# Two batches of strided attention as 32 by 32 tiles on TensorE, with a softmax of a whole unit at once and 16-bit weight conversion, in an attention and mixer kernel

## The chip, the cores and the metric

The kernel runs on one core of a Trainium2 chip. The metric is the device time of one execution in microseconds (us). Engines are named as the profile names them: PE is TensorE (PEld its weight loads), DVE is VectorE, ACT is ScalarE, POOL is GpSimd, and SP is SyncE, which here issues all DMAs.

## The reference

Eight batches of eight heads, 576 positions, head size 64. Heads 0 to 3 attend locally, heads 4 to 7 with a stride of 32; then a token mixer and a channel MLP.

```python
stride = 32
scores = scale * np.matmul(q, k.transpose(0, 1, 3, 2))
rel = pos[:, None] - pos[None, :]
mask_local = (rel >= 0) & (rel < stride)
mask_strided = (rel >= 0) & (pos[None, :] % stride == pos[:, None] % stride)
...
attn = np.exp(scores)
attn = attn / (np.sum(attn, axis=-1, keepdims=True) + 1e-09)
return np.matmul(attn, v).astype(np.float32)
...
h = np.maximum(xt @ w_tok1, 0.0) @ w_tok2
u = x + h.transpose(0, 2, 1)
h2 = np.maximum(u @ w_ch1, 0.0) @ w_ch2
return (u + h2).astype(np.float32)
```

In a strided head, the positions with the same remainder modulo 32 form a group of 18 that attends only within itself: 32 groups for each head. The weights come as 64-bit floats and are turned into 32-bit ones on the chip.

## The kernel before, in words

**The channel MLP** is most of the work. `mlp` (L450) runs nine groups of 512 tokens. In each, `up_proj(fc)` (L454) does 12 matmuls at L460 for one of 12 feature chunks, ACT makes the high part gh (L463), DVE the low part gl (L464), and `down_proj(fc)` does 12 matmuls at L472. So each product is three matmuls of split numbers (high by high, high by low, low by high), and a group is 288 matmuls. A half step is 12 of them; a group has 24. Other work hangs into the half steps by the table `ins`: the next batch's load of x (`do_load`), the token mixer (`tok1` at L336, `tok2` at L362 and L368), the local attention units of later batches (`late_unit`), the strided attention (`do_strided`), and the pieces of the weights (`do_pieces`).

**Weights.** Each piece goes through `convert` (L79) and `load_split` (L97): a DMA brings 512 KB of 64-bit numbers into one of three `w_raw` buffers; ACT takes the absolute value of the high word, rescaled, into one of two `w_f` buffers (L88); ACT copies one byte of the low word next to the high word (L92, `octets`); DVE shifts and masks (L93) and combines (L94); ACT casts to the high part (L105); POOL subtracts to get the low part (L106). There are 30 conversions: three for w_tok1, three for w_tok2 and 24 for the two channel weights.

**Local attention.** `local_unit` (L125) takes two heads and n chunks of 128 queries. Scores are matmuls of 32 queries by 64 keys (L137). Then for each chunk and head a DVE operation masks and finds the extreme (L146), and ACT takes the exponential with that as bias and sums it up on the way (L149); transposes (L160), the product with v (L167), and a division by the sums (L181). Eight units belong to batches 0 and 1 and run in the first stage, twenty later.

**Strided attention.** Batch 0 is done on PE by `strided_pe` (L217): seven groups of 18 side by side make a block of 126 by 126, of which only the diagonal is kept; per pair of heads there are ten blocks. Batches 1 to 7 are done by `strided` (L271) without PE: POOL multiplies (L286, L303), DVE reduces (L287, L305), 27 operations of each kind and batch. Their results go through DRAM (`xs`) into x.

**The order** is not the program's. The scheduler of the framework, by priorities and a timing model, sets a fixed order for each engine, and each engine then works through its queue in order. The first stage (L403 to L442) has its own pools: the `first` pool, three PSUM buffers each for local and strided work, two for the mixer. `strided` of batch 1 starts there at low priority.

## Time and profile before

| | |
|---|---|
| median of 3 runs | 879.69 us (879.41 to 881.28) |
| the profiled execution's own time | 879.49 us |
| its span, first to last instruction | 877.7 us |
| mean granted TensorE clock | 0.979 of full speed |
| busy: PE, DVE, ACT, POOL | 836.5, 482.7, 268.4, 481.3 us |

A row of groups gives line, engine and operation, what is written and read, its shape and count, then the busy time in us and the mean duration in ns, then the idle time of the engine just ahead of it and who ended it. A row of windows gives the stretch in us, then the busy time and number of instructions of PE, PEld, DVE, ACT and POOL, the granted TensorE clock (PEclk, 1.00 is full speed), the busy share of the DMA engines and GB/s. A row of a timeline starts with the time and the duration in us. Busy times of pipelined matmuls overlap, so their rate is read from the distance of their starts. A float32 matmul appears as two instructions.

### The profile page before, as it was taken

How to read it: one execution, taken by the hardware profiler on the slowest of the kernel's cores; microseconds unless marked ns; L12 is line 12 of the kernel's file. 1: busy time of each engine (PE TensorE's matmuls, PEld its weight loads, DVE VectorE, ACT ScalarE, POOL GpSimd, SP SyncE). 2: the span in 40 equal slices, each digit the busy share in tenths (PEclk: the TensorE clock that was granted, in tenths of full speed). 3: DMA queues.
4: the chain of work that ended last, by engine and by line, in shares of the span. 5: the costliest groups of instructions: out<-in, count | busy, mean ns of one | idle time of the engine just before them, and what ended most of it. 6: DMA issues, size and time to landing. Idle time of an engine off the chain costs nothing.

```text
span 877.7 us, 15029 instructions
## 1 busy us (share of the span) xinstructions
PE 836.5 (95%) x5880; PEld 666.5 (76%) x5880; DVE 482.7 (55%) x1171; ACT 268.4 (31%) x738; POOL 481.3 (55%) x453
## 2 busy tenths in 40 slices
PE   6778998899999999999999999999999999999996
PEld 5656776678777788787887887777888877888885
DVE  3999876777377746764665577557622122112112
ACT  5778667141321322122212231213212111111110
POOL 2777976979297849774795779686720002002000
PEclk9959999999998999999999999999999999999999
DMA  9557545150721351044205320521112001001001
GB/s 297 158 166 220 155 149 188 46 174 14 220 86 53 100 166 40 27 132 137 84 0 170 98 90 1 164 88 40 28 49 60 0 1 49 1 1 47 1 1 48
DMA packets 59803, 77.86 MB, mean 89 GB/s; under 512 B 20569, under 2 KB 42073, under 8 KB 59733
## 3 DMA queue, kind: packets, MB, share of 16 engines
q1 hardware_dynamic: 59732, 76.91, 28.4%
q8 instruction: 46, 0.75, 0.4%
q14 instruction: 25, 0.20, 0.1%
HBM read 58.48 MB, written 18.28 MB: 87 GB/s over the span
## 4 chain that ended last, share of the span: by engine, by line
PE 75%; DVE 10%; ACT 5%; DMA 4%; POOL 3%; issue 2%; SPq 1%; DVEq 0%; ACTq 0%; POOLq 0%
PE acc L472 29%; PE h L460 29%; PE t L368 7%; PE t L336 5%; PE t L362 3%; POOL sprod L286 3%; ACT w_raw L92 3%; DVE w_f L94 2%; DVE w_raw L93 2%; DVE xlo L328 1%; PE t L167 1%; PE t L137 1%; DVE ss L287 1%; DMA w_raw<-in_wt 1%; DMA ev<-in_vsP 1%
## 5 line engine op out<-in xcount | busy, mean ns | idle before, releaser
L286 POOL TENSOR_TENSOR sprod<-sb,sa 128x576 f32<-128x576 f32 (+6 forms) x189 | 203.7, 1106 | 94.3 <-DMA sb<-in_ks 64.1
L303 POOL TENSOR_TENSOR sprod<-sa,ss 128x448 f32<-128x448 f32 (+7 forms) x189 | 197.0, 1072 | 42.6 <-DVE ss L296 29.5
L460 PE MATMUL h<-ul,w1h 128*128 128x512 f32 x432 | 170.3, 394 | 1.3 <-DVE ul L371 1.3
L472 PE MATMUL acc<-gh,w2l 128*128 128x512 f32 x432 | 169.4, 392 | 1.3 <-POOL w2l L106 1.3
L460 PE MATMUL h<-uh,w1h 128*128 128x512 f32 x432 | 169.7, 397 | 0.5 <-DVE gl L464 0.5
L460 PE MATMUL h<-uh,w1l 128*128 128x512 f32 x432 | 169.6, 393 | 0.0
L472 PE MATMUL acc<-gl,w2h 128*128 128x512 f32 x432 | 169.5, 392 | 0.0
L472 PE MATMUL acc<-gh,w2h 128*128 128x512 f32 x432 | 165.2, 393 | 1.0 <-ACT w2h L105 0.9
L464 DVE SCALAR_TENSOR_TENSOR gl<-h,gh 128x512 fp32r<-128x512 f32 x108 | 73.7, 686 | 143.9 <-ACT gh L463 143.6
L463 ACT ACTIVATE gh<-h 128x512 fp32r<-128x512 f32 x108 | 64.4, 599 | 280.1 <-PE h L460 274.0
L287 DVE TENSOR_REDUCE ss<-sprod 128x9 f32<-128x576 f32 (+6 forms) x189 | 105.6, 569 | 65.6 <-POOL sprod L286 64.6
L488 POOL TENSOR_TENSOR ot<-ot,ul 128x512 f32<-128x512 f32 x32 | 41.0, 1291 | 174.4 <-DVE ot L486 174.4
L305 DVE TENSOR_REDUCE sb<-sprod 128x64 f32<-128x64 f32 (+8 forms) x189 | 106.3, 569 | 35.9 <-POOL sprod L303 34.5
L460 PEld LDWEIGHTS h<-ul,w1h 128*128 128x128 f32 x432 | 81.3, 188 | 19.1 <-DVE ul L371 2.1
L460 PEld LDWEIGHTS h<-uh,w1h 128*128 128x128 f32 x432 | 81.3, 189 | 18.6 <-DVE gl L464 1.2
L472 PEld LDWEIGHTS acc<-gh,w2l 128*128 128x128 f32 x432 | 81.3, 188 | 18.5 <-POOL w2l L106 2.1
L472 PEld LDWEIGHTS acc<-gh,w2h 128*128 128x128 f32 x432 | 80.9, 188 | 18.5 <-ACT w2h L105 1.7
L472 PEld LDWEIGHTS acc<-gl,w2h 128*128 128x128 f32 x432 | 81.3, 188 | 16.8
L460 PEld LDWEIGHTS h<-uh,w1l 128*128 128x128 f32 x432 | 81.3, 188 | 16.8
L149 ACT ACTIVATE ls<-ls,lm 128x64 f32<-128x64 f32 x144 | 48.1, 335 | 51.5 <-DVE lm L146 51.4
L370 ACT CAST uh<-t 128x512 fp32r<-128x512 f32 (+7 forms) x64 | 25.9, 405 | 111.9 <-PE t L368 111.8
L371 DVE TENSOR_TENSOR ul<-t,uh 128x512 fp32r<-128x512 f32 (+7 forms) x64 | 29.0, 454 | 48.1 <-ACT uh L370 47.8
(80 smaller groups left out, 994.3 us busy)
## 6 DMA issues: line engine op xcount, KB each, us to landing
w_raw<-in_w SPq DMA_DIRECT2D x24, 512.0 KB, 4.2
out_t<-ot SPq DMA_DIRECT2D x36, 256.0 KB, 2.0
x<-xs SPq DMA_DIRECT2D x8, 512.0 KB, 6.4
sa<-in_qs SPq DMA_DIRECT2D x7, 576.0 KB, 3.6
sb<-in_ks SPq DMA_DIRECT2D x7, 576.0 KB, 3.8
sa<-in_vs SPq DMA_DIRECT2D x7, 576.0 KB
xs<-sb SPq DMA_DIRECT2D x28, 144.0 KB, 2.7
lv<-in_vw SPq DMA_DIRECT2D x6, 640.0 KB, 5.4
```

Source lines behind the costliest of these rows:

```text
L149: nc.scalar.activation(out=s_t[:, c, j, :], in_=s_t[:, c, j, :], func=AF.Exp, bias=m_t[:, c, j:j + 1], scale=-1.0, accum_out=z_t[:, c, j:j ...
L286: nc.gpsimd.tensor_tensor(out=pr, in0=k_t[:, n0:n0 + n], in1=q_t[:, i:i + 1].to_broadcast([P, n, D]), op=ALU.mult)
L287: nc.vector.tensor_reduce(out=s_t[:, i, n0:n0 + n], in_=pr, axis=AX.X, op=ALU.add)
L303: nc.gpsimd.tensor_tensor(out=pr, in0=v_t[:, d0:d0 + nd, :n], in1=s_t[:, i:i + 1, :n].to_broadcast([P, nd, n]), op=ALU.mult)
L305: nc.vector.tensor_reduce(out=o_t[:, i, d0:d0 + nd], in_=pr, axis=AX.X, op=ALU.add)
L336: nc.tensor.matmul(ph[m], l, r, start=(c == 0 and k == 0), stop=(short and k == 1))
L368: nc.tensor.matmul(pu[:, :n], l[:, cs], r[:, m, t0:t1], start=False, stop=(m == 1 and k == 2), skip_group_check=True)
L460: nc.tensor.matmul(ph, l[:, cc, fs], r, start=(cc == 0 and k == 0), stop=(cc == NCC - 1 and k == 2))
L463: nc.scalar.activation(out=gh, in_=ph, func=AF.Relu)
L464: nc.vector.scalar_tensor_tensor(out=gl, in0=ph, scalar=0.0, in1=gh.bitcast(F32), op0=ALU.max, op1=ALU.subtract)
L472: nc.tensor.matmul(acc[cc], l[:, fc, cs], r, start=(fc == 0 and k == 0), stop=(fc == NFC - 1 and k == 2))
L488: add.tensor_tensor(out=o_t, in0=o_t, in1=ul.bitcast(F32), op=ALU.add)
```

## The change

- **Strided attention on PE for two batches** (`NSB = 2`, batches 0 and 1). One group of 18 is now one 32 by 32 tile: 64 score matmuls per pair of heads, into two PSUM buffers; four transposes of 128 by 128; 64 matmuls with v in two halves. `strided` remains for batches 2 to 7, and the q and k of the PE version share its `sa` and `sb` buffers.
- **Softmax of a whole unit at once**, local and strided: DVE scales and masks a whole PSUM buffer (`scalar_tensor_tensor`), one reduction finds the extremes, one operation subtracts them, one ACT instruction takes the exponential. The sums come out of the matmul with v, which has a 65th column of ones.
- **16-bit halves** in `convert`: ACT copies a 16-bit half (L87 of the new kernel) where it copied a byte, 512 elements as before.
- **The subtraction for the low part** is DVE's (`state["sub"]`) for the 14 pieces issued in the first stage (six of the token mixer, eight of the channel MLP), and POOL's for the other 16.
- **Order:** the DMA of v comes after the scores' inputs; `do_strided` of a batch is hung in at half step 14 of the group two ahead, its loads behind the load of x of the batch before; the weight pieces are inserted ahead of `do_tok2`; the PSUM pools are allocated in another order.

```diff
-        octets = raw.rearrange("p n t -> p (n t)").bitcast(U8).rearrange("p (n e) -> p n e", e=8)
-        nc.scalar.copy(out=octets[:, :n, 4], in_=octets[:, :n, 3])
-        nc.vector.tensor_scalar(out=high, in0=high, scalar1=5, scalar2=0x80000007, op0=ALU.arith_shift_right, op1=ALU.bitwise_and)
+        halves = raw.rearrange("p n t -> p (n t)").bitcast(U16).rearrange("p (n e) -> p n e", e=4)
+        nc.scalar.copy(out=halves[:, :n, 2], in_=halves[:, :n, 1])
+        nc.vector.tensor_scalar(out=high, in0=high, scalar1=13, scalar2=0x80000007, op0=ALU.arith_shift_right, op1=ALU.bitwise_and)
...
-        nc.gpsimd.tensor_tensor(out=dstl, in0=f, in1=dsth.bitcast(F32), op=ALU.subtract)
+        state["sub"].tensor_tensor(out=dstl, in0=f, in1=dsth.bitcast(F32), op=ALU.subtract)
...
-        v_t = pool.tile([P, 4 * uc, D], F32, name="lv")[:, :4 * n]
+        v_t = pool.tile([P, 4 * uc, D + 1], F32, name="lv")[:, :4 * n]
...
-        for c in range(n):
-            for j in range(2):
-                nc.vector.tensor_tensor_reduce(
...
-        nc.scalar.activation(out=z_t, in_=z_t, func=AF.Copy, bias=1e-9)
-        nc.vector.reciprocal(out=z_t, in_=z_t)
+        for j in range(2):
+            nc.vector.scalar_tensor_tensor(
+                out=s_t[:, :n, j, :], in0=sc[j][:, :64 * n].rearrange("p (c k) -> p c k", k=64), scalar=-SCALE, in1=shut,
+                op0=ALU.mult, op1=ALU.add)
+        nc.vector.tensor_reduce(out=m_t[:, :n], in_=s_t[:, :n], axis=AX.X, op=ALU.min)
+        nc.vector.tensor_tensor(
+            out=s_t[:, :n], in0=s_t[:, :n], in1=m_t[:, :n].unsqueeze(3).to_broadcast([P, n, 2, 64]), op=ALU.subtract)
+        nc.scalar.activation(out=s_t[:, :n], in_=s_t[:, :n], func=AF.Exp, scale=-1.0)
...
+        for j in range(2):
+            nc.vector.tensor_scalar_add(z_t[:, :, j:j + 1], av[j][:, :, D:], 1e-9)
+        nc.vector.reciprocal(out=z_t, in_=z_t)
...
+    def strided_pe(pool, ps_t, b, hp, qk, v_t):
+
+        sc = [ps_t.tile([P, 512], F32, name="t") for _ in range(2)]
+        for r in range(ST):
+            g, a = divmod(r, 4)
+            for j in range(2):
+                js, rs = slice(64 * j, 64 * j + 64), slice(NJ * r, NJ * r + 32)
+                nc.tensor.matmul(
+                    sc[j][32 * a:32 * a + 32, 32 * g:32 * g + 32], qk[js, rs], qk[js, S + NJ * r:S + NJ * r + 32], start=True, stop=True)
...
+        for j in range(2):
+            nc.vector.scalar_tensor_tensor(
+                out=s_t[:, 8 * j:8 * j + 8], in0=sc[j][:, :256].rearrange("p (g k) -> p g k", k=32), scalar=-SCALE,
+                in1=mask2_sb.unsqueeze(1).to_broadcast([P, 8, 32]), op0=ALU.mult, op1=ALU.add)
+        s = s_t[:, :, :NJ]
+        nc.vector.tensor_reduce(out=m_t, in_=s, axis=AX.X, op=ALU.min)
+        nc.vector.tensor_tensor(out=s, in0=s, in1=m_t.unsqueeze(2).to_broadcast([P, 16, NJ]), op=ALU.subtract)
+        nc.scalar.activation(out=s, in_=s, func=AF.Exp, scale=-1.0)
+        yield
+        pt = ps_t.tile([P, 512], F32, name="t")
+        pT = s_t.rearrange("p g k -> p (g k)")
+        for c in range(4):
+            nc.tensor.transpose(pt[:, P * c:P * c + P], pT[:, P * c:P * c + P], ident)
+        nc.scalar.copy(out=pT, in_=pt)
+        x_t = pool.tile([P, 2, 4, 2, D], F32, name="ex", bufs=1)
+        for half in range(2):
+            yield
+
+            av = [ps_t.tile([P, 512], F32, name="t") for _ in range(2)]
+            for c in range(4):
+                for a in range(4):
+                    for i in range(2):
+                        ks = slice(32 * (2 * half + i), 32 * (2 * half + i) + NJ)
+                        nc.tensor.matmul(
+                            av[i][32 * a:32 * a + 32, (D + 1) * c:(D + 1) * c + D + 1],
+                            pT[ks, P * c + 32 * a:P * c + 32 * a + 32], v_t[ks, 4 * c + a], start=True, stop=True)
+            for i in range(2):
+                k = 2 * half + i
+                o = av[i][:, :4 * (D + 1)].rearrange("p (c d) -> p c d", d=D + 1)
+                z = z_t[:, 4 * k:4 * k + 4].unsqueeze(2)
+                nc.vector.tensor_scalar_add(z, o[:, :, D:], 1e-9)
+                nc.vector.reciprocal(out=z, in_=z)
+                for j in range(2):
+                    nc.vector.tensor_tensor(
+                        out=x_t[:, :, k, j], in0=o[:, 2 * j:2 * j + 2, :D], in1=z[:, 2 * j:2 * j + 2].to_broadcast([P, 2, D]), op=ALU.mult)
...
-        strided(sp, 1, 3000)
...
-        run(*more[:2])
+        run(*more[:2], strided_pe(first, ps_s, 1, 0, *strided_load(first, 1, 0)))
         do_pieces(1)
-        run(*more[2:])
+        run(*more[2:], strided_pe(first, ps_s, 1, 1, *strided_load(first, 1, 1)))
         state["x"], state["h"] = x_t, h
         do_pieces(3)
+    state["sub"] = nc.gpsimd
...
     def do_strided(b):
-        strided(sp, b, 3000)
+
+        with tc.issue_after(state["loaded"].ins):
+            strided(sp, b, 3000)
...
-        at(HS * (b - 2) if b > 2 else 9, do_strided, b)
+        at(HS * (b - 2) + 14, do_strided, b)
```

**Where the order moves, first ACT.** These are the rows of ACT around the first gh of group 0 in the kernel before (L88, L92 and L105 belong to the conversion of a weight piece, L370 to the token mixer, L463 to the MLP):

```order
L88 ACTIVATE w_f<-w_raw 128x512
L92 COPY w_raw<-w_raw 128x512
L463 ACTIVATE gh<-h 128x512 x2
L370 CAST uh<-t 128x64
L88 ACTIVATE w_f<-w_raw 128x512
L105 CAST w1h<-w_f 128x512
L370 CAST uh<-t 128x64
L92 COPY w_raw<-w_raw 128x512
L88 ACTIVATE w_f<-w_raw 128x512
L105 CAST w2h<-w_f 128x512
L463 ACTIVATE gh<-h 128x512
```

And these are the rows of ACT at the same place in the changed kernel, where L83, L87 and L100 are the conversion, L366 the mixer and L456 makes gh:

```order
L83 ACTIVATE w_f<-w_raw 128x512
L87 COPY w_raw<-w_raw 128x512
L100 CAST w2h<-w_f 128x512 x2
L83 ACTIVATE w_f<-w_raw 128x512
L87 COPY w_raw<-w_raw 128x512
L456 ACTIVATE gh<-h 128x512 x2
L366 CAST uh<-t 128x64 x2
L100 CAST w2h<-w_f 128x512
L456 ACTIVATE gh<-h 128x512
L366 CAST uh<-t 128x64 x2
L456 ACTIVATE gh<-h 128x512
L323 CAST xh<-x 128x512 x2
```

In the kernel before, 16 of the 30 conversions stand ahead of the first gh on ACT, and 14 between later ones. In the changed kernel all 30 stand ahead of it, all but the last cast.

**Second, PE at the start of group 0.** In the kernel before, these rows lie ahead of the first down projection (L472) on PE; L460 is the up projection, L362 and L368 the mixer for the rest of batch 0:

```order
L460 MATMUL h<-ul,w1h 128x512
L460 MATMUL h<-uh,w1l 128x512
L362 MATMUL t<-ident,x 128x64
L368 MATMUL t<-t2h,hh_113 128x64
L368 MATMUL t<-t2l,hh_113 128x64
```

In the changed kernel these rows lie at the same place, between the first 24 up projections (L453) and the mixer (L358): the transposes and products of the last strided unit of batch 1 (L239, L250) and of the last local units (L157, L164):

```order
L453 MATMUL h<-uh,w1l 128x512
L239 MATMUL t<-ident,es 128x128 x4
L157 MATMUL t<-ident,ls 128x128 x2
L164 MATMUL t<-lv,ls 32x65 x16
L250 MATMUL t<-ev,es 32x65 x32
L164 MATMUL t<-lv,ls 32x65 x16
L250 MATMUL t<-ev,es 32x65 x32
L358 MATMUL t<-ident,x 128x64
```

Ahead of the first down projection PE has the same attention of batches 0 and 1 behind it in both kernels, except that the strided heads of batch 1 have joined it.

More of the change, by code (lines that the diff above doesn't have):

```diff
@@ L31 @@
 LC = 5
[L32 to L36 removed]
+NSB = 2
 NCC = DM // P
@@ L240, in strided_pe @@
         yield
         pt = ps_t.tile([P, 512], F32, name="t")
-        pT = s_t
-        for i, r in enumerate(rows):
-            nc.tensor.transpose(pt[:r, RP * i:RP * i + r], s_t[:r, i, :r], ident[:r, :r])
-        nc.scalar.copy(out=pT[:, :nf], in_=pt[:RP, :RP * nf].rearrange("p (c k) -> p c k", k=RP))
-        if nf < n:
-            r = rows[nf]
-            nc.scalar.copy(out=pT[:r, nf, :r], in_=pt[:r, RP * nf:RP * nf + r])
-        yield
-        av = ps_t.tile([P, 512], F32, name="t")
@@ L536, in late_unit @@
             at(i0 + k, go)
-    for g in range(B):
-        at(HS * g + 1, do_tok2, g, True)
     for i in range(16):
```

152 lines of the change are left out of this document (55 added, 97 removed).

## The prediction

> **What bounds the kernel now.** I read the page first, then the busy times by stage.
>
> ```profile
> span 877.7 us, 15029 instructions
> PE 836.5 (95%) x5880; PEld 666.5 (76%) x5880; DVE 482.7 (55%) x1171; ACT 268.4 (31%) x738; POOL 481.3 (55%) x453
> ```
>
> The windows by stage, with the busy us of PE, PEld, DVE, ACT and POOL, then PEclk, DMA share and GB/s:
>
> ```profile
> 0.00:45.00 45.00, 31.56 (x389) 25.31 (x390) 28.69 (x132) 31.64 (x125) 24.22 (x30) 1.00 0.73 229
> 45.00:95.00 50.00, 40.86 (x436) 30.80 (x436) 47.20 (x129) 39.95 (x101) 39.15 (x34) 0.76 0.60 184
> 95.00:179.00 84.00, 76.69 (x362) 59.37 (x362) 62.01 (x102) 46.32 (x74) 65.43 (x55) 0.98 0.41 128
> 179.00:274.00 95.00, 94.32 (x928) 73.51 (x927) 61.18 (x174) 27.64 (x102) 65.96 (x66) 1.00 0.40 120
> 274.00:286.00 12.00, 10.11 (x71) 7.60 (x71) 9.31 (x27) 2.65 (x7) 12.00 (x11) 0.72 0.17 66
> 286.00:870.00 584.00, 582.96 (x3702) 469.89 (x3700) 271.39 (x611) 120.23 (x335) 274.53 (x262) 1.00 0.19 59
> ```
>
> From 179 us on PE is the bound: it idles under 4 us in 691, and the stretch at a low clock in 274 to 286 is the only other loss. A cheaper softmax there buys nothing. Up to 95 us DVE is the bound (47.2 of 50 us in the second window). From 95 to 179 us group 0 of the MLP runs beside the last conversions of weights. So two things can change: when group 0 starts, and how densely it runs. The timeline of PE gives the marks: the first down projection, the two stretches of mixer inside group 0 (each by its first row and the first row behind it), and the first matmul of group 1. The chain shows an undisturbed run of matmuls (start, us, what):
>
> ```profile
> 95.48 0.48 PE L472 MATMUL acc<-gh,w2h 128*128 128x512 f32 x1
> ...
> 101.65 0.27 PE L362 MATMUL t<-ident,x 64*128 64x64 f32 x1
> ...
> 103.53 0.48 PE L460 MATMUL h<-ul,w1h 128*128 128x512 f32 x1
> ...
> 173.93 0.27 PE L362 MATMUL t<-ident,x 128*128 128x128 f32 x1
> ...
> 176.67 0.50 PE L472 MATMUL acc<-gl,w2h 128*128 128x512 f32 x1
> ...
> 179.07 0.39 PE L460 MATMUL h<-uh,w1h 128*128 128x512 f32 x1
> ```
> ```profile
> 796.16 7.93 PE acc L472 x35
> ```
>
> One matmul takes 7.93/35 = 0.227 us. After the first 24 up projections group 0 has 288 − 24 = 264 matmuls, and the mixer's first product for batch 1 has 28: 292 × 0.227 = 66.2 us. The two stretches of mixer and scores take 103.53 − 101.65 = 1.9 and 176.67 − 173.93 = 2.7, or 4.6 us. That is 70.8 us of work in 179.07 − 95.48 = 83.6 us: **12.8 us are lost** while group 0 runs among conversions. This is what the change can win, and a later first down projection is what it can pay.
>
> **The change part by part.**
>
> *Order on ACT and DVE.* ACT works in order, so gh waits for all 30 conversions where it waited for 16. The first down projection now comes when the conversions are done, T1, against 95.5 before. After T1 nothing of the weights is left, so the 12.8 us go. I charge 1.5 us there for matmuls at a low clock behind the wait, and 1 us for the boundary to group 2, where PE order now has no down projections between the mixer's products. The nearest row for both is this wait, behind which the clock stood low (window 274 to 286, 0.72):
>
> ```profile
> 278.25 0.47 PE L362 MATMUL t<-ident,x 128*128 128x128 f32 x1 [1.89 <-DVE hl L340]
> ```
>
> So the new span is 877.7 + (T1 − 95.5) − 12.8 + 2.5, and the change breaks even at T1 = 105.8. All hangs on T1.
>
> *The conversion on ACT.* Rows of ACT:
>
> ```profile
> L92 ACT COPY w_raw<-w_raw 128x512 uint8<-128x512 uint8 x28 | 38.1, 1371 | 0.3
> L88 ACT ACTIVATE w_f<-w_raw 128x512 f32<-128x512 f32 x28 | 19.0, 679 | 4.0 <-POOL w1l L106 1.6 <-DMA w_raw<-in_wt 1.2 <-POOL w2l L106 0.8
> L105 ACT CAST w1h<-w_f 128x512 fp32r<-128x512 f32 x12 | 7.5, 622 | 7.4 <-DVE w_f L94 7.4
> L149 ACT ACTIVATE ls<-ls,lm 128x64 f32<-128x64 f32 x144 | 48.1, 335 | 51.5 <-DVE lm L146 51.4
> L149 ACT ACTIVATION_READ_ACCUMULATOR ls<-ls,lm 128x1 f32 x144 | 26.9, 187 | 0.0
> ```
>
> The 16-bit copy is not in this trace. Its bounds are 0.62 (a 512-element cast) and 1.37 us (the byte copy); a gain is the only sign that excludes neither. I take 0.62, as rows with 32-bit elements on both sides (0.679 even at a stride of two) are all near it. [...] ACT up to T1: 30 × (0.68 + 0.62 + 0.62) = 58 us, and some 19 us for exponentials, copies and casts (36 local ones at 0.335 + 0.187 become eight of 0.4 to 0.5): 77 us, or 99 with the slow copy.
>
> *DVE up to T1.* Rows of groups, then two pairs of single operations, without and with POOL at work:
>
> ```profile
> L94 DVE SCALAR_TENSOR_TENSOR w_f<-w_f,w_raw 128x512 uint32<-128x512 uint32 x28 | 31.9, 1138 | 0.6
> L93 DVE TENSOR_SCALAR w_raw<-w_raw 128x512 uint32<-128x512 uint32 x28 | 18.6, 664 | 12.7 <-ACT w_raw L92 12.6
> L371 DVE TENSOR_TENSOR ul<-t,uh 128x512 fp32r<-128x512 f32 x8 | 5.5, 684 | 10.3 <-ACT uh L370 10.3
> L287 DVE TENSOR_REDUCE ss<-sprod 128x9 f32<-128x576 f32 (+6 forms) x189 | 105.6, 569 | 65.6 <-POOL sprod L286 64.6
> L305 DVE TENSOR_REDUCE sb<-sprod 128x64 f32<-128x64 f32 (+8 forms) x189 | 106.3, 569 | 35.9 <-POOL sprod L303 34.5
> ```
> ```profile
> 24.44 0.41 DVE L93 TENSOR_SCALAR w_raw<-w_raw 128x512 uint32<-128x512 uint32 x1
> 24.77 0.68 DVE L94 SCALAR_TENSOR_TENSOR w_f<-w_f,w_raw 128x512 uint32<-128x512 uint32 x1
> 25.38 0.67 DVE L287 TENSOR_REDUCE ss<-sprod 128x8 f32<-128x512 f32 x1
> ...
> 35.27 1.70 DVE L94 SCALAR_TENSOR_TENSOR w_f<-w_f,w_raw 128x512 uint32<-128x512 uint32 x1
> ```
>
> Starts lie 0.08 us closer than durations (24.77 + 0.68 − 25.38). Batch 1 leaves: 54 reductions × 0.569 = 31 us. New: 14 subtractions × 0.68 = 10; four strided units at about 5 us, from 0.41 to 0.68 for each 256 to 512 elements and 0.2 to 0.3 for the 32 small ones; the local units stay near 2.6 each. In sum 30 × (0.41 + 0.68) + 10 + 20 + 21 + 8 for the mixer = 92 us, less 248 × 0.08 = 72 us. POOL now does only 16 subtractions here, so an L94 at 1.70 us becomes rare; I add 5 us. The Trainium skill, "SBUF — State Buffer", SBUF: two separate sides, says that POOL and DVE share a port pair under a lock held for a whole instruction. By that, as an estimate, the 16 could hold DVE for up to 16 times the duration of one, some 20 us in place of 5; the rows show only the mean, 1.138 against 0.68 us, with POOL busy through most of it.
>
> *Buffers and DMA.*
>
> ```profile
> w_raw<-in_w SPq DMA_DIRECT2D x24, 512.0 KB, 4.2
> ```
> ```profile
> 4.00:8.00 4.00, 1.38 (x68) 1.17 (x72) 0.00 (x0) 0.00 (x0) 0.00 (x0) 1.00 0.92 315
> ```
>
> Counted by the tiles in its queue, SP has 26.8 MB to issue up to the last weight: at 315 GB/s 85 us. A `w_raw` buffer is filled again when DVE is through with it: 4.2 from issue to landing, 0.68 + 0.62 on ACT, 0.41 + 0.68 on DVE, and by estimate 0.9 for the issue and the hops between engines, 7.5 us; with three buffers 2.5 us a piece.
>
> *T1.* The first weights can land near 17 us (4.3 MB stand ahead of them, 14 us at that rate, begun near 3). From there 30 pieces at 2.5 are 75 us, so T1 is not under 17 + 75 + 2 = 94 by the buffers, 87 by DMA, 82 to 97 by the engines. Four limits that close do not all run full where each engine works in order. In the second window DVE, first by over 6 us, ran at 47.2/50 = 94%; here none is so clearly first, and I take 2.7 us a piece: 17 + 30 × 2.7 + 2, T1 = **100 us**, with 92 and 106 as bounds.
>
> *The strided units on PE.*
>
> ```profile
> L137 PE MATMUL t<-lk,lq 64*32 64x64 f32 x1152 | 22.3, 241 | 8.3 <-DMA lk<-in_kT 6.6 <-DVE lm L146 1.3 <-DVE lx L181 0.2
> L167 PE MATMUL t<-lv,ls 64*32 64x64 f32 x1152 | 19.4, 235 | 0.1
> L229 PE MATMUL t<-ek,eq 64*126 64x126 f32 x32 | 8.3, 445 | 2.4 <-DVE ss L287 1.3 <-DVE em L232 1.0
> L253 PE MATMUL t<-ev,es 126*126 126x64 f32 x32 | 8.1, 423 | 1.1 <-ACT es L248 0.7 <-DVE ex L257 0.3
> ```
>
> Narrow tiles run side by side: 22.3 us/1152 = 19 ns each, against 8.3/32 = 260 ns for a wide block. Four units have 4 × 256 instructions × 19 ns = 19 us and 16 transposes; the 126-wide blocks of batch 0 took over 16 us in these two rows alone. So PE's load hardly changes, and it lies ahead of T1, under the conversions. If 32 rows ran no better than wide blocks: 1024 × 0.26 = 266 us.
>
> *Costed at nothing:* the 65th column (within PE's stage of local units, one column in 64), the larger local softmax after T1 (gl waits at most one operation), POOL's relief in group 0, and the later strided batches: about 75 us each for a group of over 85, begun right behind the load of the batch before. If that cover failed, the mixer of a batch would wait for `xs`.
>
> **The rivals.**
>
> 1. *The 16-bit copy is as slow as the byte copy* (0.25). ACT then paces the block: 3.4 us a piece from 32 us, where the 24 pieces of the MLP begin, gives T1 = 32 + 24 × 3.4 = 113.6, behind 105.8, and a span of 885.5: **887 us**. For it speaks the byte row, more than twice any other of 512 elements; against it, that no other type shows this. It decides from 3.05 us a piece.
> 2. *The block is slow for another cause* (0.09): hops, SP's queue, or tiles. T1 past 108: 882 to 895 us.
> 3. *Group 0 starts as early as before* (0.15): conversions at 2.4 us, T1 = 90 to 95. The span falls to 862 to 867: **866 us**.
> 4. *No change* (0.09): T1 within 1.8 us of 105.8.
>
> **How the numbers follow.** My forecast (0.42) is T1 = 100: 877.7 + 4.5 − 12.8 + 2.5 = 871.9 of span. The profiled execution's own time is 1.8 us over its span (879.49), and 0.2 under the median of the runs (879.69): 873.7, say **873.5 us**. Its own range is 867 to 878. Over the cases, 861 to 890 leaves out the fastest part of the third rival and the worst of the second. A measurement of this kernel tells 0.2% (1.8 us) from no change. Faster 0.42 + 0.15 = 0.57, same 0.09, slower 0.25 + 0.09 = 0.34.
>
> **What would show it.** Right: the first down projection near 100 us, 70 to 73 us from there to group 1, the copy near 0.62, DVE over 80% busy up to T1, and PE full from T1 on. Wrong: a copy near 1.37; a down projection past 106; group 0 as thin as before; strided matmuls over 40 ns apart; waits for `xs` in later groups.

## The result, and the profile after

| | before | changed |
|---|---|---|
| median | 879.55 us (878.81 to 881.28, 4 runs) | 917.47 us (916.20 to 917.49, 3 runs) |
| ratio | | 1.0423, 95% interval 1.0402 to 1.0445 |
| profiled execution: span | 877.7 us | 914.3 us |
| first down projection, T1 | 95.5 us | 122.0 us |
| T1 to the first up projection of group 1 | 83.6 us | 78.5 us |
| group 1 | 104.5 us | 109.5 us |
| from group 2 to the end | 594.1 us | 604.3 us |

The kernel is 4.2% slower; the forecast was 0.7% faster. The ratio is that of the means of the undisturbed executions; the one that was profiled with the result was disturbed (1,625.8 us), so the profile read here is of the same kernel run once more, 916.24 us. Its page:

```profile
span 914.3 us, 16320 instructions
PE 851.5 (93%) x6820; PEld 673.9 (74%) x6820; DVE 467.4 (51%) x973; ACT 221.7 (24%) x393; POOL 402.5 (44%) x384
```

DVE, ACT and POOL all have less work than before (15, 47 and 79 us less), and the time is 36.6 us longer. PE is 15 us busier with the same MLP. The windows by stage, in the columns of the prediction, cut at the new marks:

```profile
0.00:45.00 45.00, 20.98 (x715) 17.16 (x716) 24.72 (x77) 25.48 (x41) 1.01 (x7) 1.00 0.82 260
45.00:95.00 50.00, 39.70 (x761) 30.80 (x764) 38.26 (x120) 40.58 (x64) 9.10 (x7) 0.86 0.73 235
95.00:122.00 27.00, 16.44 (x317) 12.81 (x304) 17.14 (x52) 21.57 (x31) 11.09 (x8) 0.73 0.49 148
122.00:200.00 78.00, 78.00 (x404) 62.17 (x405) 44.73 (x84) 12.85 (x25) 50.17 (x51) 0.96 0.18 59
200.00:310.00 110.00, 102.05 (x904) 78.68 (x904) 61.21 (x124) 19.99 (x40) 62.35 (x61) 0.95 0.35 107
310.00:900.00 590.00, 588.05 (x3721) 467.63 (x3721) 276.31 (x512) 101.18 (x194) 268.77 (x253) 1.00 0.19 58
```

Up to 45 us POOL and half of PE stand idle; from 45 to 122 no engine is full, ACT being the busiest (62 of 77 us; DVE 55). From 122 to 200 us and from 310 us on PE is full; in group 1, between them, it is busy for 102 of 110 us. So the span divides into T1 +26.5, group 0 −5.1, group 1 +5.0 and the rest +10.2: 36.6 us. Against the forecast it is 22.0 on T1, 6.2 on group 0 (72.3 forecast), 4.0 on group 1 (105.5), and 10.2 on a rest that was given no term.

The mark between groups 0 and 1 has moved as well. A stretch of mixer and scores of 2.8 us lies ahead of it here (197.58 to 200.39) and behind it in the kernel before (179.69 to 182.48). The two groups together are the safer number: 188.0 us against 188.1 before, so they won nothing, where the forecast was 177.8.

The last of the first 24 up projections of the kernel before, then of the changed kernel ACT's timeline at the end of the conversions, and PE's from that last up projection to the first down projection:

```profile
93.27 0.40 PE L460 MATMUL h<-uh,w1l 128*128 128x512 f32 x1
```
```profile
119.44 0.66 ACT L83 ACTIVATE w_f<-w_raw 128x512 f32<-128x512 f32 x1
120.13 1.36 ACT L87 COPY w_raw<-w_raw 128x512 uint16<-128x512 uint16 x1
121.21 1.19 ACT L456 ACTIVATE gh<-h 128x512 fp32r<-128x512 f32 x2
```
```profile
102.13 0.39 PE L453 MATMUL h<-uh,w1l 128*128 128x512 f32 x1
103.34 0.66 PE L239 MATMUL t<-ident,es 128*128 128x128 f32 x4 [0.82 <-ACT es L234]
...
107.77 1.19 PE L250 MATMUL t<-ev,es 18*32 18x65 f32 x64 [2.97 <-ACT es L240]
...
112.92 1.09 PE L250 MATMUL t<-ev,es 18*32 18x65 f32 x32 [1.87 <-DVE ex L260]
115.69 0.34 PE L358 MATMUL t<-ident,x 64*128 64x64 f32 x1 [1.68 <-issue]
...
118.76 0.40 PE L364 MATMUL t<-t2h,hl 128*128 128x64 f32 x1
121.97 0.80 PE L465 MATMUL acc<-gh,w2h 128*128 128x512 f32 x1 [2.81 <-DVE w_raw L88]
```

Of T1's 26.5 us, 8.9 lie ahead of that last up projection (102.13 against 93.27) and 17.6 behind it (19.8 to T1, against 2.2). The up projections were done at 102.5 us. gh could not be made before 121.21, behind the thirtieth conversion on ACT (PE's releaser is named a conversion's, though what it waits for is gh behind it). But PE waited for gh only in the last 2.81 of those 19 us. Ahead of that it did the last strided unit of batch 1 and the mixer behind it, waiting for small steps that stand between conversions on ACT and DVE. ACT's queue and PE's own both hold T1.

### The profile page after: what moved, and what is told of

Same layout as the page of the kernel before. It is cut to its first block, busy times and chain, and to the rows that moved or that the text cites. A ratio compares the mean times of both kernels' runs of the same rounds, so it can differ in the third digit from the quotient of the medians.

```text
span 1624.0 us, 16320 instructions
## 1 busy us (share of the span) xinstructions
PE 1575.1 (97%) x6820; PEld 1018.4 (63%) x6820; DVE 462.8 (28%) x973; ACT 222.4 (14%) x393; POOL 395.6 (24%) x384
## 4 chain that ended last, share of the span: by engine, by line
PE 93%; ACT 2%; DMA 2%; DVE 2%; issue 1%; SPq 0%; DVEq 0%; ACTq 0%
PE h L453 37%; PE acc L465 37%; PE t L364 7%; PE t L332 6%; PE t L358 2%; PE t L132 1%; ACT w_raw L87 1%; PE t L164 1%; PE t L157 1%; ACT w_f L83 1%; DMA sb<-in_qksT 1%; DMA out_t<-ot 1%; DVE w_f L89 0%; DMA w_raw<-in_w 0%; DMA w_raw<-in_wt 0%
## 5 line engine op out<-in xcount | busy, mean ns | idle before, releaser
L453 PE MATMUL h<-uh,w1l 128*128 128x512 f32 x432 | 292.8, 678 | 0.0
L453 PE MATMUL h<-ul,w1h 128*128 128x512 f32 x432 | 292.1, 676 | 0.0
L465 PE MATMUL acc<-gl,w2h 128*128 128x512 f32 x432 | 291.9, 676 | 0.0
L465 PE MATMUL acc<-gh,w2l 128*128 128x512 f32 x432 | 291.3, 674 | 0.0
L453 PE MATMUL h<-uh,w1h 128*128 128x512 f32 x432 | 288.1, 675 | 0.0
L465 PE MATMUL acc<-gh,w2h 128*128 128x512 f32 x432 | 284.3, 675 | 3.0 <-ACT gh L456 3.0
L465 PEld LDWEIGHTS acc<-gl,w2h 128*128 128x128 f32 x432 | 130.1, 301 | 71.7 <-issue 66.7
L465 PEld LDWEIGHTS acc<-gh,w2l 128*128 128x128 f32 x432 | 129.9, 301 | 68.8 <-issue 62.7
L456 ACT ACTIVATE gh<-h 128x512 fp32r<-128x512 f32 x108 | 64.5, 599 | 791.0 <-PE h L453 791.0
L453 PEld LDWEIGHTS h<-uh,w1l 128*128 128x128 f32 x432 | 129.3, 299 | 68.6 <-issue 63.6
L453 PEld LDWEIGHTS h<-uh,w1h 128*128 128x128 f32 x432 | 128.5, 298 | 67.4 <-issue 61.4
L453 PEld LDWEIGHTS h<-ul,w1h 128*128 128x128 f32 x432 | 126.3, 292 | 67.4 <-issue 61.4
L282 DVE TENSOR_REDUCE ss<-sprod 128x9 f32<-128x576 f32 (+6 forms) x162 | 88.9, 569 | 44.6 <-POOL sprod L281 44.4
L300 DVE TENSOR_REDUCE sb<-sprod 128x64 f32<-128x64 f32 (+8 forms) x162 | 88.9, 568 | 23.9 <-POOL sprod L298 23.2
L366 ACT CAST uh<-t 128x512 fp32r<-128x512 f32 (+7 forms) x64 | 26.0, 408 | 296.2 <-PE t L364 296.2
L364 PE MATMUL t<-t2h,hh 128*128 128x512 f32 (+7 forms) x128 | 64.2, 501 | 0.0
```

The source lines that it names most:

```text
L282: nc.vector.tensor_reduce(out=s_t[:, i, n0:n0 + n], in_=pr, axis=AX.X, op=ALU.add)
L300: nc.vector.tensor_reduce(out=o_t[:, i, d0:d0 + nd], in_=pr, axis=AX.X, op=ALU.add)
L364: nc.tensor.matmul(pu[:, :n], l[:, cs], r[:, m, t0:t1], start=False, stop=(m == 1 and k == 2), skip_group_check=True)
L453: nc.tensor.matmul(ph, l[:, cc, fs], r, start=(cc == 0 and k == 0), stop=(cc == NCC - 1 and k == 2))
L456: nc.scalar.activation(out=gh, in_=ph, func=AF.Relu)
L465: nc.tensor.matmul(acc[cc], l[:, fc, cs], r, start=(fc == 0 and k == 0), stop=(fc == NFC - 1 and k == 2))
```

## The experiments

T1 and the two stretches behind it are read from PE's timeline of each run; times with an interval are medians of several rounds beside the kernel before (879.3 to 880.6 us there), the others single. Each kernel was scheduled anew, so the order of other instructions can move a little with each edit.

### The conversion: the copy

**Changed kernel again.** No edit.

> The changed kernel unchanged, for a profile of an execution at about 916 us. Theory A (the conversions): all 30 conversions at a copy of 1.37 us stand ahead of the first gh, so the first down projection comes at 112 to 125 us (95.5 before) and group 0 then takes under 75 us, as nothing is converted beside it; by that alone the time would be 887 to 900 us. Theory B (later stages): the MLP groups 1 to 8 themselves are slower than before, by over 15 us in sum, by idle PE or a lower granted clock; then the time from the first matmul of group 1 to the end is over 715 us against 698.6 before. Both can hold; A alone leaves over 15 us of the 38 unexplained.

916.24 us, the slower time again, with the copy at 1.366 us and T1 at 122.0. The profile above is this run's.

**The 16-bit half alone, in the kernel before.**

```diff
...
-        nc.scalar.copy(out=octets[:, :n, 4], in_=octets[:, :n, 3])
...
+        nc.scalar.copy(out=halves[:, :n, 2], in_=halves[:, :n, 1])
...
```

> The kernel before with only the copy of a 16-bit half in place of a byte. Theory A: the copy's time goes by something other than its type, 1.36 to 1.37 us as the byte's, and the time is that of before within 0.2% (878 to 881 us). Rival: the type counts in this place and the copy in the changed kernel was slowed by other work; then it takes under 1.1 us here and the time falls by 2 to 5 us.

878.79 us, ratio 0.9995 (0.9976 to 1.0014). The groups of the copy, first in the changed kernel, then here:

```profile
L87 ACT COPY w_raw<-w_raw 128x512 uint16<-128x512 uint16 x28 | 38.2, 1366 | 0.5
```
```profile
L92 ACT COPY w_raw<-w_raw 128x512 uint16<-128x512 uint16 x28 | 38.2, 1374 | 0.3
```

The byte copy had taken 1.371 us. A half is no cheaper: this edit does nothing, and the copy lies at the upper of the prediction's two bounds, not at the 0.62 us that it took.

**No copy** (the lowest three bits of a converted weight are left out; everything else stands).

```diff
-        nc.scalar.copy(out=halves[:, :n, 2], in_=halves[:, :n, 1])
```

> The changed kernel without ACT's copy of the 16-bit halves; it leaves out the lowest three bits of the converted weights, and DVE's work is as before. The prediction's own sum: with a copy of 0 us ACT is no limit, and the first down projection would come at 100 us or earlier; if ACT's 1.37 us a piece is what was mis-sized, it now comes at 95 to 106 us and the last conversion starts before 102 (122 and 119.4 with the copy). Rival L (DVE's order and the mixer hold the first down projection, whatever ACT has to do): it comes at 112 to 122 us.

905.93 us. The end of the conversions, and the first down projection:

```profile
102.40 0.70 ACT L83 ACTIVATE w_f<-w_raw 128x512 f32<-128x512 f32 x1
```
```profile
112.87 0.40 PE L363 MATMUL t<-t2h,hl 128*128 128x64 f32 x1
113.08 1.20 PE L464 MATMUL acc<-gh,w2h 128*128 128x512 f32 x2
```

The last conversion starts 17 us earlier (102.40 against 119.44), T1 only 9 (113.1 against 122.0). Now PE does not wait for gh at all: its down projection follows the mixer's last product at its usual distance. The copy is about 10 us of the loss; behind it PE's own queue, with the tail of batch 1's attention, holds T1 at 113. And 30 conversions still take 2.95 us each, (102.40 − 16.75)/29 from the start of the first to that of the last, where they took (119.44 − 17.34)/29 = 3.5.

**The copy done by DVE** (three operations on DVE in place of two and ACT's copy).

```diff
-        nc.scalar.copy(out=halves[:, :n, 2], in_=halves[:, :n, 1])
-        nc.vector.tensor_scalar(out=high, ..., scalar1=13, scalar2=0x80000007, ...)
+        nc.vector.tensor_scalar(out=low, in0=low, scalar1=29, scalar2=None, op0=ALU.logical_shift_right)
...
+        nc.vector.scalar_tensor_tensor(out=a, in0=high, scalar=0x80000000, in1=a, op0=ALU.bitwise_and, op1=ALU.bitwise_xor)
```

> The changed kernel without ACT's copy: DVE shifts the low word right by 29 in place, combines it with the rest, and puts the sign on in a third operation, so ACT loses 1.37 us a conversion and DVE gains 0.7 to 0.8. Theory A: ACT paces the conversions, the first down projection comes 12 to 25 us earlier, and the time falls to 892 to 905 us. Theory B: what is lost lies in later groups, and the time stays within 912 to 917. Rival C: DVE was as near to its limit as ACT, the pace stays and the time is 915 to 925.

927.48 us, ratio 1.0536 (1.0502 to 1.0569), T1 130.2. Its window from 45 to 95 us:

```profile
45.00:95.00 50.00, 33.32 (x597) 25.51 (x597) 44.98 (x117) 23.88 (x48) 11.92 (x7) 0.88 0.71 219
```

DVE went from 38.26 to 44.98 us of 50 and is now by far the fullest engine: worse.

### Who else could hold T1

**More buffers**, four for the loads in one kernel, three `w_f` in the other (`ot`, and in the first `gl` too, give one up each to make room).

```diff
-        raw = stage.tile([P, DM, 2], U32, name="w_raw", bufs=3)
+        raw = stage.tile([P, DM, 2], U32, name="w_raw", bufs=4)
```
```diff
-        a = stage.tile([P, DM], U32, name="w_f", bufs=2)[:, :n]
+        a = stage.tile([P, DM], U32, name="w_f", bufs=3)[:, :n]
```

> The changed kernel with four buffers w_raw instead of three; the room is taken from the pool of gh (gl in two buffers instead of three, ot in one instead of two), so only the stage up to the first down projection can be read. Theory G (the cycle of a buffer paces the conversions: 3.4 us a piece from 20 to 121 us, or 10 us for each of three buffers, and SP waits 35 us for DVE to release one): a piece takes 2.7 to 3.0 us and the first down projection comes at 106 to 114 us. Rival H (the operations behind each other on ACT and DVE pace them): it comes at 118 to 123 us.

> The changed kernel with three buffers w_f instead of two (ot in one buffer instead of two, so only the stage up to the first down projection can be read). A piece holds its w_f from ACT's first operation to the subtraction: 0.68 + 1.37 on ACT, 0.43 + 0.81 on DVE, 0.62 on ACT, 0.68 on DVE or 1.3 on POOL, with hops and queues about 6 to 7 us, so two buffers give 3 to 3.5 us a piece, which is what is measured (102 us for 29). Theory I (w_f paces the conversions): with three the last conversion starts at 95 to 108 instead of 119 us. Rival H (the two engines in order, each behind the other's other work): the last conversion starts at 115 to 120 us as before.

T1 122.7 and 124.3 us (times 925.83 and 927.91; what lies behind T1 also has fewer `ot` and `gl`, so only T1 is read). With four buffers for the loads the last conversion starts at 113.78, with three `w_f` at 107.92, 5.7 and 11.5 us earlier than in the changed kernel, and T1 is no earlier: the up projections come later (the last at 108.6 and 108.7), and behind the attention's tail and the mixer PE reaches its first down projection without a wait. Both buffers slow the conversions, but the end of the conversions alone does not move T1.

**The subtractions back on POOL.**

```diff
-    state = {"sub": nc.vector}
+    state = {"sub": nc.gpsimd}
```

> The changed kernel with every subtraction for a low part on POOL, as in the kernel before (14 of 30 were DVE's). Theory A: DVE loses 14 x 0.68 = 9.5 us of work, but w_f is held 0.6 us longer and L89 meets more POOL work (0.81 to 1.1 us a piece): the first down projection at 118 to 124 us, time 912 to 920 us, so this part of the change is worth nothing either way. Rival: DVE paces the conversions and the first down projection comes at 112 us or earlier.

925.55 us, T1 128.8. Having them on DVE was good for 7 us of T1 (single runs): this part of the change pays.

**gh ahead of 12 pieces of weights.** The pieces of half steps 4 to 15 are bound behind the first gh.

```diff
-            nc.scalar.activation(out=gh, in_=ph, func=AF.Relu)
+            ins = nc.scalar.activation(out=gh, in_=ph, func=AF.Relu)
+            state.setdefault("gh", ins)
...
+    def late_piece():
+        with tc.issue_after(state["gh"].ins):
+            do_pieces(1)
...
-        at(i, do_pieces, 1)
+        at(i, *((do_pieces, 1) if i < 4 else (late_piece,)))
```

> The changed kernel with the last 12 pieces of weights bound behind the first gh on ACT: 18 conversions stand ahead of it (30 in the changed kernel, 16 before), PE's order is unchanged. Theory A in the form that the place in ACT's queue decides: gh comes as soon as its matmuls are done (102.5 us), PE then has the tail of batch 1's attention and the mixer ahead of its first down projection, so this comes at 110 to 117 us instead of 122; group 0 is then thinned out by 12 conversions and takes 80 to 86 us instead of 78.5, and the time is 908 to 918 us. Rival F (the mixer's rest and PE's own order hold the down projection, not gh): it stays within 1.5 us of 122 and the time is 918 to 928.

905.8 us, ratio 1.029 (1.0248 to 1.0332). The scheduler then puts 18 conversions ahead of the first gh. PE's timeline from the last up projection to the mark:

```profile
96.05 0.40 PE L453 MATMUL h<-uh,w1l 128*128 128x512 f32 x1
...
105.02 0.40 PE L364 MATMUL t<-t2h,hl 128*128 128x64 f32 x1
105.23 2.05 PE L466 MATMUL acc<-gh,w2h 128*128 128x512 f32 x4
```

T1 comes 16.7 us earlier (105.23 against 121.97), and group 0 is hardly thinner for the 12 conversions inside it: group 1 begins at 182.36, so it takes 77.1 us, against 75.7 in the changed kernel without the stretch of 2.8 us, which here lies in group 1. PE again goes from the mixer straight to the down projection. The attention tail, too, runs with ACT and DVE freer: from the last up projection to the first down projection 9 us, where it took 20. Of the 17 us, groups 0 and 1 give back 3.4 (191.4 against 188.0).

**Batch 1's strided heads back on POOL and DVE.**

```diff
-NSB = 2
+NSB = 1
...
+        strided(sp, 1, 3000)
```

> The changed kernel with batch 1's strided heads given back to POOL and DVE (NSB = 1, strided(1) at low priority ahead of the last local units); batch 0 stays in 32 by 32 tiles. 26 conversions then stand ahead of the first gh. Theory A: two strided units less on ACT's queue and PE, 4 conversions less ahead of gh, but 31 us of reductions on DVE: first down projection 5 to 15 us earlier, group 0 some 5 us longer, 905 to 915 us. Rival D: the tiles of batch 1 and their tail between the conversions are the cause; then the time falls to 885 us or less. Theory B: over 912.

922.28 us, ratio 1.0477 (1.0448 to 1.0506): T1 121.2, group 1 116.7. The tail behind the last up projection is short here (7.9 us), but that projection comes at 113.4. So taking batch 1 to PE is not what moved T1 on balance, and it is worth some 5 us of the time where it stands.

**The tiles alone, for batch 0, in the kernel before** (its `strided_pe` and `strided_load` replaced by the changed kernel's; local softmax, order and copy as before).

```diff
-        sc = ps_t.tile([P, 512], F32, name="t")
+        sc = [ps_t.tile([P, 512], F32, name="t") for _ in range(2)]
...
-        x_t = pool.tile([P, max(n - 1, 2) if into is not None or n == 2 else uc, 2, D], F32, name="lx")
+        x_t = pool.tile([P, max(n - 1, 2) if into is not None or n == 2 else uc, 2, D], F32, name="lx", bufs=1)
```

> The kernel before with the 32 by 32 tiles for batch 0 alone, in place of its 126 by 126 blocks (lx in one buffer, q and k of a unit in one tile; old local softmax, byte copy, POOL's subtractions, batch 1 on POOL and the old times); tiles and weights start at the same address modulo 512. 20 conversions stand ahead of the first gh instead of 16. Against the blocks ACT loses some 15 us of 17 ahead of the first down projection, DVE nothing (about 10.5 us for two units against 11), PE 16 wide pairs of products. Theory O (DVE was the bound up to there, 47.2 of 50 us): the first down projection stays between 94 and 102 us, group 0 has 10 instead of 14 conversions beside it and takes 80 to 84 us, and the time is 874 to 884 us. Rival (ACT and the chain of the blocks were as much a bound): it comes at 86 to 93 us and the time falls below 872. Rival (4 more conversions ahead of gh cost more than the tiles win): over 103 us and above 885.

892.14 us, ratio 1.0129 (1.0102 to 1.0156), T1 113.0 with 20 conversions ahead of the first gh where 16 stood. PE's timeline before that mark:

```profile
76.67 0.73 PE L456 MATMUL h<-uh,w1h 128*128 128x512 f32 x2 [1.75 <-ACT uh L368]
...
102.58 0.50 PE L456 MATMUL h<-uh,w1h 128*128 128x512 f32 x1 [0.50 <-ACT uh L368]
...
112.83 0.40 PE L366 MATMUL t<-t2h,hl 128*128 128x64 f32 x1
113.04 2.05 PE L468 MATMUL acc<-gh,w2h 128*128 128x512 f32 x4
```

Even the headline part, cheap as its matmuls are, does not pay in the order that the scheduler makes of it: the first twelve up projections begin at 76.7 where they began at 74.7, but the second twelve at 102.6 where they began at 88.9.

### The local softmax of a whole unit

**It alone, in the kernel before** (the changed kernel's `local_unit`, with the 65th column, its mask and one buffer `lx` in place of two).

```diff
-        for c in range(n):
-            for j in range(2):
-                nc.vector.tensor_tensor_reduce(
...
+        nc.vector.tensor_reduce(out=m_t[:, :n], in_=s_t[:, :n], axis=AX.X, op=ALU.min)
```

> The kernel before with the new softmax of the local units alone (whole units at once, 65th column, lx in one buffer); strided attention, conversions and order of before; tiles and weights start at the same address modulo 512. 19 conversions stand ahead of the first gh instead of 16. Theory M (the softmax's part is good: ACT loses 36 operations of 0.52 us up to the first down projection, and nothing else is changed): 872 to 879 us. Rival K (its operations on DVE stand behind reductions that wait for POOL and hold PE at the mixer of batch 2): group 1 takes 108 us or more against 104.5, and the time is 881 to 890.

910.74 us, ratio 1.0357 (1.0336 to 1.0377): T1 +12.7, group 1 +11.0, the rest +7.1. DVE's groups of the softmax up to 108 us, before and, the larger ones, in this run (8.8 of the 9.3 us idle are the wait for the mask):

```profile
L146 DVE CUSTOM_DVE_ANT_0 ls<-t,mask_sb 128x64 f32<-128x64 f32 x36 | 5.9, 214 | 9.3 <-DMA mask_sb<-in_mask 8.8 <-PE t L137 0.5
```
```profile
L154 DVE TENSOR_TENSOR ls<-ls,lm 128x256 f32<-128x256 f32 x6 | 6.4, 1075 | 0.0
L150 DVE SCALAR_TENSOR_TENSOR ls<-t,mask_sb 128x128 f32<-128x128 f32 x12 | 3.1, 275 | 0.0
L153 DVE TENSOR_REDUCE lm<-ls 128x4 f32<-128x256 f32 x6 | 2.4, 401 | 0.0
L176 DVE TENSOR_SCALAR lz<-t 128x2 f32<-128x2 f32 x12 | 1.5, 147 | 0.2 <-PE t L170 0.2
```

The eight units take 6.4 + 3.1 + 2.4 + 1.5 = 13.4 us of DVE, and 1.2 + 1.1 + 1.1 in the same lines at larger shapes: 16.8 us, and a little more in smaller rows, for 5.9 us (and 36 short reads of the extremes, most of them beside other operations). One operation that masks and reduces has become three passes over the same numbers. ACT gains by it (one exponential for many), but DVE is the fullest engine here (47.65 of 50 us from 45 to 95).

**It taken out of the changed kernel** (`local_unit` of before, its mask, its two buffers `lx`, v loaded ahead of the scores, no 65th column).

```diff
-        nc.vector.tensor_reduce(out=m_t[:, :n], in_=s_t[:, :n], axis=AX.X, op=ALU.min)
...
+        for c in range(n):
+            for j in range(2):
+                nc.vector.tensor_tensor_reduce(
```

> The changed kernel with the local softmax of the kernel before (one DVE operation and one accumulating exponential for each chunk and head, no 65th column in the local units), all else of the change as it is; addresses modulo 512 as in the changed kernel (0 and 128). 28 conversions stand ahead of the first gh instead of 30. The softmax alone cost the kernel before 31 us: 17.3 us instead of 5.9 on DVE ahead of the first down projection, 12.7 us there, 11 in group 1 and 7 later. Theory N (the same here): the time falls from 916.5 to 885 to 900 us, and group 1 takes 100 to 105 us (109.5 in the changed kernel). Rival (here ACT and the place of gh set the first down projection, and DVE has room, 39 of 50 us): under 5 us are won at the start, and the time stays at 905 to 914.

905.56 us, ratio 1.0299 (1.0261 to 1.0338): T1 119.0, group 0 75.4, group 1 104.7, where the kernel before has 104.5. Groups 0 and 1 together take 180.0 us, 8.0 less than in the changed kernel. So the loss in group 1 is this softmax, and at T1 it is only 3 us here, where it was 12.7 alone. Its single buffer `lx` is not the cause: the tiles alone, above, have one too, and their groups 0 and 1 take 183.9 us. In group 1 PE's waits sum to 7.9 us in the changed kernel and to 3.0 with the old softmax. The longest (line waited for, us, times, longest) from 200 to 310 us, with the rows of ACT, DVE and PE that bear on it:

```profile
PE t L332 <- DVE lx L180: 3.5, 1, 3.5
```
```profile
254.39 1.14 ACT L323 CAST xh<-x 128x512 fp32r<-128x512 f32 x2 [6.95 <-DMA x<-xl]
```
```profile
288.67 0.55 DVE L300 TENSOR_REDUCE sb<-sprod 128x64 f32<-128x384 f32 x1 [0.48 <-POOL sprod L298]
289.14 1.28 DVE L479 TENSOR_TENSOR ot<-acc,uh 128x512 f32<-128x512 f32 x2
290.33 1.35 DVE L300 TENSOR_REDUCE sb<-sprod 128x64 f32<-128x448 f32 x2
291.60 0.22 DVE L170 TENSOR_SCALAR lz<-t 128x4 f32<-128x4 f32 x2
292.09 0.76 DVE L180 TENSOR_TENSOR lx<-t,lz 128x256 f32<-128x256 f32 x2
```
```profile
292.66 0.76 PE L332 MATMUL t<-xh,t1h 128*128 128x512 f32 x1 [3.54 <-DVE lx L180]
```

The mixer at L332 is batch 2's, and its first inputs were cast at 254.39 already. What it waits for are the PSUM buffers `t`: there are two, and the products of the last local unit of batch 3 (four chunks, hence 128x4) hold both until DVE has divided them. That division (L170, L180) stands on DVE behind strided reductions that themselves wait for POOL.

### The rest: where tiles lie in SBUF

PE in the rest has the same matmuls at a granted clock of 1.00, yet one is slower. The chain has 12 at a time, here in group 8 of the kernel before and of the changed one:

```profile
856.00 2.72 PE acc L472 x12
858.72 2.72 PE h L460 x12
```
```profile
892.31 2.79 PE acc L465 x12
895.11 2.73 PE h L453 x12
```

In odd groups of the changed kernel both are slower, here in group 7:

```profile
800.68 2.80 PE h L453 x12
803.48 2.80 PE acc L465 x12
```

The addresses are those of the built programs; no trace shows them. In the kernel before the weights, gh, gl and u all begin at 384 modulo 512 bytes. In the changed one the weights and the u of even groups are at 0, and gh, gl and the u of odd groups at 128, so the slower rows are those in which the tile streamed through PE (gh, gl or u) starts elsewhere than the weights.

**384 unused bytes ahead of the MLP's tiles, in the changed kernel; 128 in the kernel before** (there `[P, 32]`). The order of the instructions stays the same.

```diff
+    ctx.enter_context(tc.tile_pool(name="gap", bufs=1)).tile([P, 96], F32, name="pad")
     up = ctx.enter_context(tc.tile_pool(name="up", bufs=3, reuse_waits="tile"))
```

> The changed kernel with 384 unused bytes in front of the pool that holds gh, gl and the u of odd groups; the order of every engine is unchanged. In the kernel before, these tiles and the weights start at the same address modulo 512 (384 and 384); in the changed kernel at 128 and 0, while the u of even groups starts at 0 as the weights do. Theory D (addresses): the matmuls that read a moving tile from there are paced at 0.234 us instead of 0.227, which makes 1.0 us for each 144, so 9 x 1.0 for the down projections and 4 x 1.0 for the up projections of odd groups, 13 us; with the shift the pace in the last group is 0.227 throughout and the time is 900 to 906 us. Rival E (PSUM banks: the change allocates h, acc and t in other banks): nothing changes, 915 to 918 us.

> The kernel before with 128 unused bytes in front of the same pool, so gh, gl and the u of odd groups start at 0 modulo 512 and the weights at 384; the order of every engine is unchanged, and so are the PSUM banks. Theory D: the down projections slow to 0.234 us a matmul, and the time rises by 10 to 15 us, to 890 to 895. Rival E: no change, 878 to 881 us.

907.19 us, ratio 1.0297 (1.0276 to 1.0318), the rest 597.0 for 604.3; and, the other way, 888.3 us, ratio 1.0083 (1.0059 to 1.0107), the rest 601.8 for 594.1. The same rows, of the shifted changed kernel and of the shifted kernel before:

```profile
883.85 2.72 PE acc L466 x12
886.57 2.72 PE h L454 x12
```
```profile
864.44 2.79 PE acc L473 x12
867.23 2.73 PE h L461 x12
```

An empty tile takes the loss from one kernel and gives it to the other, with the places in PSUM as they were. That is 7 of the 10.2 us of the rest. The other kernels here fall in line: where all these tiles start alike (the softmax alone, the tiles alone, the cures below) both rows take 2.72 us in group 8, and where they are at 0 and 128 (no copy, gh ahead, old softmax) 2.79 and 2.73. That the place within 512 bytes is what counts, and not the place otherwise, was read from these layouts only.

### Cures together

Four kernels, all with gh ahead and the 384 bytes. The second takes the kernel before's times for the strided batches, the third only for batches 3 to 7, the fourth has the old local softmax. The strided batches that are moved back no longer wait for the load of x, either:

```diff
-        at(HS * (b - 2) + 14, do_strided, b)
+        at(HS * (b - 2) if b > 2 else 9, do_strided, b)
```
```diff
-        at(HS * (b - 2) + 14, do_strided, b)
+        at(HS * (b - 2) + (14 if b == 2 else 0), do_strided, b)
```

> The changed kernel with both cures: 18 conversions ahead of the first gh, and the 384 unused bytes. If the two causes are apart, their gains add: 905.8 - 10.3 = 895.5 us, 892 to 899. If the gain of the earlier gh were due to the pace of matmuls, or the other way round, the time stays above 901.

> The same as the kernel with both cures, with the strided attention of batches 2 to 7 hung in at the half steps of the kernel before (9 of group 0 for batch 2, the start of the group two ahead for the others) and its loads no longer behind the load of x. Theory J (the later start is what group 1 loses: PE waits 7 to 10 us around the mixer of batch 2): the time falls by 5 to 9 us against the kernel with both cures, to 887 to 891. Rival K (DVE's order, with more softmax on it, makes these waits): no gain, or a loss of up to 8 us because reductions that wait for POOL now stand ahead of batch 1's attention on DVE, and the first down projection comes later than 106 us.

> The kernel with both cures (899.8 us), with the strided attention of batches 3 to 7 hung in at the start of the group two ahead as in the kernel before, batch 2's at half step 14 as in the changed kernel. In the run with all times of before, group 1 took 108.7 us instead of 114.4 while group 0 took 86.9 instead of 78.2. Theory J in this form (each effect belongs to its own batch): group 0 stays at 77 to 80 us, group 1 falls to 107 to 110, and the time is 892 to 897. Rival: group 1 stays over 112 and the time at 897 to 903.

> The same with both cures: 18 conversions ahead of the first gh, and tiles and weights at the same address modulo 512. So what stays of the change are the 32 by 32 tiles for two batches, the subtractions on DVE, the 16-bit halves and the order. If the three causes are apart: 899.8 us less 10 to 25, 875 to 890 us. If the softmax cost only where DVE was full (in the kernel before), 893 to 900. The kernel before stands at 880.

| | T1 | group 0 | group 1 | rest | us | ratio |
|---|---|---|---|---|---|---|
| both cures | 105.5 | 78.2 | 114.4 | 599.0 | 899.82 | 1.0231 (1.0192 to 1.027) |
| and strided times of before | 109.9 | 86.9 | 108.7 | 597.2 | 909.4 | 1.0317 (1.0283 to 1.0351) |
| and batches 3 to 7 early | 104.6 | 78.6 | 115.8 | 610.6 | 911.91 | 1.0368 (1.0328 to 1.0408) |
| both, and old softmax | 108.4 | 77.6 | 107.3 | 601.2 | 893.1 | 1.0164 (1.0136 to 1.0192) |

Alone the two cures take off 11.7 and 10.3 us, together 17.7. The runs with gh ahead spread by some 3.5 us to each side, so the 4 us short of the sum are hardly clear of noise. The stretch of 2.8 us lies in group 0 in the second row and in group 1 in the others; allowing for it, the old times of the strided batches give group 1 back 2.9 us and cost 5.9 in group 0, where their POOL and DVE work then lies. With batch 2 late and the others early, group 1 gains nothing and the rest loses 11.6, which was not expected; PE waits 10.8 us there, most of it for DVE, and 4.6 with both cures alone. The old softmax takes off 6.7 us more. What is left over the kernel before is, in the profiled spans, T1 +12.9, group 0 −6.0, group 1 +2.8 and the rest +7.1: 16.8 us (13.6 in the medians). No kernel here beats the one before.

## Why the prediction was wrong

- **T1 = 17 + 30 × 2.7 + 2 = 100.** This is the step that failed, by 22 us: the pace of a conversion, and that T1 is the end of the conversions. The first conversion starts at 17.3, as forecast, but a piece takes 3.5 us. *The 16-bit copy at 0.62 us* is one cause: it takes 1.366, so 30 × 0.75 = 22 us of ACT were missing; without the copy T1 is 113.1 and the time some 10 us less. The rival that named this (887 us) had this mechanism and its sign right and was still 30 us short. *The pace from the busier engine* is the second, as with no copy at all a piece takes 2.95 us. *T1 is when the conversions are done* holds only in part. With the copy left out, or gh put ahead, or more buffers, the first down projection follows PE's own mixer with no wait (113.1, 105.2, 122.7 and 124.3). The order shown ahead of the prediction has the strided and local products between the up and down projections on PE, and the prediction gave them no time; they and the mixer take 7 to 22 us there, by how soon ACT and DVE serve them.
- **DVE and ACT paced by 94% of the busier one.** The trace has ACT at 62 (81%) and DVE at 55 of 77 us from 45 to T1. In that time DVE waited 20.3 us for ACT's copies and ACT 9.5 us for what DVE hands back: a conversion goes through ACT, DVE and ACT again, and small steps of the attention wait in both queues between. The sum for DVE itself was near: 80.1 us busy up to T1 for 72 + 5. But that is 66% of the time, not the "over 80%" named as a sign.
- **"The local units stay near 2.6 each" on DVE.** As a term this came out right, 20.1 us for the eight against 21, but not by its reason: the old ones take some 12 us in the kernel before, apart from the short reads, so the units did not "stay". Put into the kernel before, this softmax moved T1 by 12.7 us; taken out of the changed kernel, by 3.0.
- **The 12.8 us of group 0.** More of it came than the marks show. Without the stretch of 2.8 us group 0 takes 75.7, against 83.6 before and 72.3 forecast. Of the 6.2 us over the forecast the stretch is 2.8, and the slower matmuls are 1.0: 12 pairs of half steps at 2.79 + 2.73 in place of 2 × 2.72. The low clock behind the wait was charged 1.5 us and took 3.0: these 24 matmuls take 8.43 us, where 24 × 0.227 = 5.45 (the granted clock is 0.84 from 122 to 140 us).

```profile
121.97 2.08 PE acc L465 x4
124.05 4.50 PE h L453 x12
128.55 1.85 PE acc L465 x8
```

  That the conversions inside group 0 thin it was hardly borne out: with 12 of them inside, and no other edit, group 0 took 77.1 us, 1.4 more. In the kernel before PE waited 5.2 us of that group for the mixer's split inputs, and only 2.2 for converted weights.
- **"Costed at nothing".** The larger local softmax after T1 was to delay gl by one operation. It costs 8 us in groups 0 and 1; without it they take 180.0 us, near the 177.8 of the forecast. The cover named, PE's full queue, was there for gl; it was not for the PSUM buffers `t`, which the mixer shares with the local units. The later strided batches: PE did not wait for `xs`, but their reductions stand ahead of `lx` on DVE.
- **The rest, no term at all.** +10.2 us, of which 7 are the place of the tiles in SBUF, which a diff of pools and shapes decides and no row of before could show.
- **What was right.** The strided units on PE: 64 matmuls in 1.19 us (the row at 107.77) are 18.6 ns each, for 19 forecast. That T1 is the largest term. That PE would not wait for `xs`.

**Open.** Why T1 stays at 105 to 113 once the copy or the order is mended is argued from PE's queue, not shown by an order without the attention's tail there, which was not tried. In the rest of the kernel with the local softmax alone PE waits 5.0 us, 0.5 in the kernel before, which leaves 2.6 of its 7.1 us unexplained; of the 7.1 us of the last of the cures, and of the 11.6 us of the early strided batches, some 5 each are not explained.

## What to carry to other kernels

When several engines share a stage, count what each new form costs on the engine that is the bound there: three plain passes on DVE in place of one that masks and reduces cost more than the exponentials they saved. When an order moves, follow every instruction between the last producer and the mark on the engine itself; the mark may hang on its own queue and not on the wait that the diff makes visible. And when a steady loop of the same matmuls changes its pace, look at where its tiles start before looking for waits.
